# Linear attention and a two-layer MLP on one core: the hand-written order of chunks 0 to 2 is made anew

## The chip, the core and the metric

The kernel runs on one core of a Trainium2 chip. Its engines work side by side, each through its own instructions in order: TensorE (PE, matrix products into PSUM), VectorE (DVE), ScalarE (ACT), GpSimd (POOL, which also issues some of the DMAs) and SyncE (SP, which issues the other DMAs). An engine waits where its next instruction needs something that another engine or a transfer has not yet delivered. The metric is the device time of one execution in microseconds (us): 216.57 us is the median of three timed runs (216.57 to 217.8).

## The reference

Two stages, the second on the first's output (4 batches, 8 heads, 768 positions, head size 64; the MLP has 3072 tokens, 512 inputs and 2048 hidden columns):

```python
for b in range(nb):                       # blocks of 64 positions, one after the other
    intra = einsum('bhic,bhjc->bhij', qb, kb) * Dmask          # lam ** (i - j), 0 above the diagonal
    intra = einsum('bhij,bhjd->bhid', intra, vb)
    inter = einsum('bhid,bhde->bhie', qb * lam_pow, kv_state)
    out[:, :, sl] = intra + inter
    kv_state = lam_block * kv_state + einsum('bhsd,bhse->bhde', kb * rev_pow, vb)
h = x @ w_in                              # x: out, heads side by side, 3072 x 512
g = maximum(h, 0.0) + alpha * minimum(h, 0.0)
return g @ w_out                          # 3072 x 512
```

All inputs and the output are float32; the kernel multiplies in float16.

## The kernel before

**Chunks and units.** The work is cut into six chunks `c` of 512 tokens: 256 positions (two blocks of 128) of two batches `bi`. `pb = c // 2` is the place in the sequence; chunks 0 and 1 hold the first positions of all four batches. A chunk has four attention units (`units`, numbered 4c to 4c+3): batch 0 or 1 of the chunk, with the first or the second four heads. So units 4 to 7 are chunk 1: 4 and 5 of its first batch, 6 and 7 of its second.

**A unit's steps.** `load` (line 80) brings q, k or v of one batch of a chunk (0.5 MB, or half of it) from HBM, issued on SP. `cast` (line 261) makes float16 of it for one unit; a letter names the engine: A is ACT, V is DVE, G is POOL. `key_decayed` (line 274) multiplies k by its decay. `transposes` (line 291) brings q and k head size first: eight PE transposes and a copy from PSUM bank tk, or, with "D", one DMA transpose issued on SP. `transposed` (line 317) does q or k alone. `decayed` (line 335) multiplies the transposed q by its decay. `cluster(old, new)` (line 350) is PE's part: the inter and intra products of unit `old` and the scores and the state of unit `new`, then DVE's masked scores `sm`, the state update (R on ACT or DVE, RD on ACT for the first positions and on POOL later) and the copy of the output into `xT`. Either side may be absent.

**The MLP's steps.** `up(c, f)` (line 474) is four matmuls of 512 columns that make 128 of the 2048 hidden columns for a chunk, then ACT's `m` (line 487) and DVE's product `g` (line 503, at once, or later by `slope_product`). It needs all four units' `xT` and a quarter of w_in (`f // 4`). `down(c, t, part, 4)` (line 512) is four of the sixteen matmuls for 128 output tokens; `part` is the quarter of w_out that it reads. Behind the last part ACT copies the sum (line 531) and SP stores it, at once or by `store_held`.

**PSUM.** Banks by name: "h" (two), "op", "tk", and others for the clusters. A new user of a bank waits until the earlier one's readers are done.

**Weights.** `load_win(i)` (line 95) and `load_wout(i)` (line 101) bring a quarter of w_in or w_out, cast to float16 on the way, and are issued on POOL, where they stand in order with its casts and products. `gate` (line 109) is a tiny DMA on SP that reads one element of a weight quarter: SP waits in it until that quarter has landed, and so holds back the loads behind it:

```python
w = w_in_sb[0:1, 0, i * 512 : i * 512 + 1] if which == "in" else w_out_sb[0:1, 4 * i, 0:1]
nc.sync.dma_start(out=gates16[:, x : x + 1], in_=w)
```

**The order.** It is written out by hand, line by line, from line 595 on: the opening (chunk 0's attention, with `fill` matmuls of no use to the result that keep PE at work), then chunk 0's `up` and `down` with chunk 1's attention between, then chunk 1's `up` with chunk 2's attention. From line 817 a loop over chunks weaves the rest: `up` of chunk c and `down` of chunk c - 1 alternate, with the attention of chunk c + 1 spread among them.

```python
for c in range(2, NC):
    ...
    for f in range(NF):
        moe.append(lambda f=f: up(c, f))
        moe.append(lambda f=f: down(c - 1, f // 4, f % 4, 4))
    weave(att, moe)
```

The last chunk's `down` stands at the end (`down_last`).

Of the kernel before, what the change touches and what calls it, by code (L numbers as in the profile page):

```python
# [11 lines left out]
def kernel(  # L12
# [24 lines left out]
    B, H, S, D = q.shape  # L37
# [3 lines left out]
    NC = (S // W) * 2  # L41
# [88 lines left out]
    def fill(n, bank="h", zeros=None, w=CH):  # L130

        t = bank_of(bank, "unread")
        for i in range(n * CH // w):
            if w < CH:
                x = ident if zeros is None else zeros[:, 0:128]
                nc.tensor.matmul(t[:, ds(i * w % CH, w)], lhsT=x, rhs=x[:, 0:w], start=True, stop=True)
                continue
            if zeros is not None:
                nc.tensor.matmul(t, lhsT=zeros[:, 0:128], rhs=zeros, start=True, stop=True)
                continue  # L140
            nc.tensor.matmul(
                t.rearrange("p (a j) -> p a j", a=4),
                lhsT=ident,
                rhs=ident.unsqueeze(1).to_broadcast([128, 4, 128]),
                start=True,
                stop=True,
            )
# [322 lines left out]
    G = {}  # L470
# [3 lines left out]
    def up(c, f, bi=None, bank="h", later=False):  # L474
        h_ps = bank_of(bank, "h_ps")
        n = CH if bi is None else W
        for gi in range(NHP):
            x = XT[c][:, gi]
            nc.tensor.matmul(  # L479
                h_ps[:, 0:n] if bi is None else h_ps[:, 0:n].rearrange("p (e j) -> p e j", e=2),  # L480
                lhsT=w_in_sb[:, gi, ts(f, 128)],
                rhs=x.rearrange("p e b j -> p (e b j)") if bi is None else x[:, :, bi, :],
                start=(gi == 0),
                stop=(gi == NHP - 1),
            )
# [191 lines left out]
    up(0, 1, None, "op")  # L677
    up(0, 4, None, "tk", True)
    slope_product(0, 4, None)
    up(0, 3, None, "h", True)  # L680
    key_decayed(4, "G")
    slope_product(0, 3, None)
    cast(5, "k16", "G")
    up(0, 6, None, "h", True)
    up(0, 2, None, "op")
    up(0, 7, None, "tk")
    slope_product(0, 6, None)
    cast(4, "q16", "A")
    up(0, 5, None, "h")
    up(0, 8, None, "op")  # L690
    up(0, 11, None, "tk")
    up(0, 10, None, "h")
    load_wout(1)
    cast(4, "v16", "A")
    gate(3, "in")
    up(0, 14, None, "h")
    up(0, 15, None, "op")
    up(0, 13, None, "h")
    transposes(4, "V", False)
    decayed(4, "P")  # L700
    gate(1, "out")
    up(0, 9, None, "h")
    up(0, 12, None, "op")
# [6 lines left out]
    cast(6, "k16", "G")  # L710
    down(0, 2, 0, 4, "op")
    cast(6, "q16", "V")
    load_wout(2)
    transposes(6, "A", False)
    key_decayed(5, "G")
    down(0, 0, 1, 4, "h")
    load(2, 0, "k", None)
    cast(5, "v16", "V")
    key_decayed(6, "V")
    cast(7, "q16", "A")  # L720
    down(0, 2, 1, 4, "op")
    decayed(6, "G")
    load(2, 0, "q", None)
    cast(7, "k16", "V")
    load_wout(3)
    cluster(4, 5, "V", state_first=True)
    load(2, 1, "k", None)
    cast(8, "q16", "G")
    transposes(7, "A", False)
    decayed(5, "V")  # L730
    down(0, 3, 1, 4, "h")
    down(0, 3, 2, 4, "h")
    cast(9, "q16", "G")
    cast(6, "v16", "V")
    down(0, 2, 2, 4, "op")
    decayed(7, "V")
    cluster(5, 6, "A", state_first=True)
    key_decayed(8, "G")
    down(0, 1, 0, 4, "tk")
    down(0, 1, 1, 4, "tk")  # L740
    down(0, 1, 2, 4, "tk")
    key_decayed(7, "V")
    load(2, 0, "v", None)
    cast(8, "k16", "V")
    key_decayed(9, "V")
    transposes(8, "D", False)
    cast(9, "v16", "G")
    cast(7, "v16", "A")
    cluster(6, 7, "V", state_first=True)
    down(0, 0, 2, 4, "h")  # L750
    down(0, 0, 3, 4, "h")
    key_decayed(10, "V")
    cast(9, "k16", "G")
    load(2, 1, "q", None)
    down(0, 2, 3, 4, "op", True)
    cluster(7, None, "A")
    cast(8, "v16", "V")
    transposes(9, "D", False)
    cast(10, "k16", "G")
    down(0, 3, 3, 4, "h", True)  # L760
    up(1, 0, None, "h")
    query_decay(1, 0)
    store_held(0, 3)
    decayed(8, "G")
    up(1, 12, None, "op", True)
    slope_product(1, 12, None)
    up(1, 6, None, "h", True)
    slope_product(1, 6, None)
    load(2, 1, "v", None)
    cluster(None, 8)  # L770
    key_decayed(11, "G")
    query_decay(2, 0)
    decayed(9, "G")
    up(1, 1, None, "h", True)
    slope_product(1, 1, None)
    cast(11, "k16", "A")
    up(1, 7, None, "op", True)
    cast(10, "q16", "A")
    transposes(10, "D", False)
    slope_product(1, 7, None)  # L780
    cast(11, "q16", "A")
    down(0, 1, 3, 4, "tk")
    up(1, 13, None, "h", True)
    load(3, 0, "q", None)
    cluster(8, 9, "A")
    transposes(11, "D", False)
    slope_product(1, 13, None)
    load(3, 0, "k", None)
    decayed(10, "G")
    up(1, 2, None, "tk", True)  # L790
    slope_product(1, 2, None)
    up(1, 3, None, "op")
    store_held(0, 2)
    cast(10, "v16", "A")
    up(1, 15, None, "h", True)
    cluster(9, 10, "A")
    slope_product(1, 15, None)
    up(1, 10, None, "tk", True)
    load(3, 0, "v", None)
    cast(11, "v16", "A")  # L800
    load(3, 1, "k", None)
    slope_product(1, 10, None)
    up(1, 11, None, "h")
    up(1, 9, None, "op", True)
    decayed(11, "G")
    cluster(10, 11, "A")
    up(1, 5, None, "tk")
    up(1, 14, None, "h")
    slope_product(1, 9, None)
    up(1, 4, None, "h", True)  # L810
    slope_product(1, 4, None)
    cluster(11, None, "A")
    load(3, 1, "v", None)
    load(3, 1, "q", None)
    up(1, 8, None, "tk")
# [42 lines left out]
```

## Time and profile before

| What | Value |
|---|---|
| Timed runs, median | 216.57 us |
| The profiled execution | 215.89 us, span 214.1 us |
| Granted clock of TensorE | 0.999 |
| PE busy | 205.5 us, 96% of the span |
| DVE, ACT, POOL busy | 61%, 54%, 41% |
| HBM read and written | 27.27 MB, 6.29 MB |
| First `up` matmul | 20.20 us |
| Last of PE's matmuls starts | 210.6 us |

How to read it: times in the timeline count from the start of the span. A row gives start and length, the engine, the line of the kernel, the operation, what is written and read, and the number of instructions of the row; brackets give the idle time ahead of the first and what ended it. "q" behind an engine's name is its sequencer, which issues a DMA or waits. A DMA's landing is when its completion was seen, which is later than its last packet. Matmuls are pipelined, so the length of a row of them goes a little beyond the start of the next one; PE's pace is read from start to start (0.216 us for 512 columns). Queue q0 carries the loads that POOL issues (the weights), q1 those of SP. The shares of the DMA queues are of 16 DMA engines, and go over 100% where packets overlap.

### The profile page before, as it was taken

What the parts mean: (1) busy time and instruction counts of PE and PEld (TensorE: products, weight loads), DVE (VectorE), ACT (ScalarE), POOL (GpSimd) and SP (SyncE); (2) the same over time, 40 slices, a digit from 0 to 9 for tenths busy, and PEclk for the clock granted to TensorE, in tenths of its full rate; (3) what the DMA queues carried; (4) which work ended last, traced back from release to release, by engine and by line L of the source; (5) the groups of instructions that cost most, each with busy time, mean ns of one, the idle gap of its engine ahead of it and who ended that gap; (6) DMA issues with size and microseconds to landing.
All of it is one profiled execution on the core that took longest, in us unless ns stands there. A gap on an engine that the chain in (4) does not pass through costs nothing.

```text
span 214.1 us, 5232 instructions
## 1 busy us (share of the span) xinstructions
PE 205.5 (96%) x2093; PEld 107.5 (50%) x2093; DVE 129.6 (61%) x254; ACT 115.6 (54%) x218; POOL 87.7 (41%) x163
## 2 busy tenths in 40 slices
PE   7779997999999999999999999999999999999993
PEld 7455444555455444555554554554554444444453
DVE  7867689487799947676655655655546344444000
ACT  6978687245787654646554554644534543444121
POOL 8175056203775644976967357358301000000000
PEclk9999999999999999999999999999999999999999
DMA  5999999999999999699387786044011101110212
GB/s 148 298 277 194 226 299 218 183 263 261 218 207 296 316 221 259 166 239 230 77 210 183 198 222 173 0 101 98 5 49 49 39 13 51 49 49 3 98 49 98
DMA packets 62478, 33.90 MB, mean 158 GB/s; under 512 B 18150, under 2 KB 59510, under 8 KB 62454
## 3 DMA queue, kind: packets, MB, share of 16 engines
q1 hardware_dynamic: 58182, 29.37, 54.2%
q0 software_dynamic: 4224, 4.19, 12.0%
q8 instruction: 16, 0.26, 0.5%
q14 instruction: 8, 0.07, 0.1%
q10 hardware_dynamic: 48, 0.01, 0.0%
HBM read 27.27 MB, written 6.29 MB: 157 GB/s over the span
## 4 chain that ended last, share of the span: by engine, by line
PE 72%; DMA 20%; POOL 3%; SPq 2%; issue 1%; ACT 1%; ACTq 0%; POOLq 0%
PE h_ps L479 30%; PE o_ps L518 29%; DMA w_out_sb<-in_moe_w_out_dram 8%; PE o_ps L547 6%; DMA w_in_sb<-in_moe_w_in_dram 4%; DMA kraw<-in_k_dram 3%; DMA vraw<-in_v_dram 3%; PE s L384 2%; DMA qkT<-qk 2%; PE acc L396 2%; PE acc L367 2%; SPq L87 1%; POOL qk L252 1%; POOL qdT L340 1%; PE acc L411 1%
## 5 line engine op out<-in xcount | busy, mean ns | idle before, releaser
L503 DVE SCALAR_TENSOR_TENSOR g<-m,oma,h_ps 128x512 f16<-128x512 f32 (+1 forms) x97 | 70.6, 741 | 58.0 <-ACT m L487 57.1
L479 PE MATMUL h_ps<-xT,w_in_sb 128*128 128x512 f16 (+1 forms) x388 | 94.8, 377 | 0.0
L487 ACT ACTIVATE m<-h_ps 128x512 f32<-128x512 f32 (+1 forms) x97 | 57.3, 592 | 57.8 <-PE h_ps L479 55.1
L518 PE MATMUL o_ps<-w_out_sb,g 128*128 128x512 f16 x320 | 80.9, 379 | 1.2 <-DMA w_out_sb<-in_moe_w_out_dram 1.1
L479 PEld LDWEIGHTS <-w_in_sb 128*128 128x128 f16 x388 | 37.1, 98 | 43.0
L518 PEld LDWEIGHTS <-g 128*128 128x128 f16 x320 | 30.2, 98 | 36.2 <-issue 1.6
L422 DVE TENSOR_TENSOR sm<-s,dmask 128x512 f16<-128x512 f32 x48 | 30.8, 683 | 5.4 <-PE s L384 5.0
L461 POOL COPY RD<-R 64x128 f16<-64x128 f16 x64 | 18.5, 288 | 36.3 <-DVE R L447 33.8
L340 POOL TENSOR_TENSOR qdT<-qkT,qdecay 128x512 f16<-128x512 f16 (+1 forms) x20 | 21.2, 1062 | 12.4 <-ACT qkT L248 5.7
L531 ACT ACTIVATE o_sb<-o_ps 128x512 f32<-128x512 f32 (+2 forms) x26 | 14.7, 564 | 16.9 <-PE o_ps L547 10.9
L248 ACT ACTIVATE xT<-acc 128x512 f16<-128x512 f32 x22 | 13.1, 596 | 10.4 <-PE acc L411 7.2
L278 POOL TENSOR_TENSOR kdec<-kraw,kdecay 128x512 f16<-128x512 f32 x17 | 17.8, 1045 | 0.1
L252 POOL CAST qk<-kraw 128x512 f16<-128x512 f32 x20 | 12.1, 610 | 11.1 <-DMA kraw<-in_k_dram 10.3
L547 PE MATMUL o_ps<-w_out_sb,g 128*128 128x512 f16 (+2 forms) x96 | 14.1, 308 | 0.0
L447 DVE SCALAR_TENSOR_TENSOR R<-R,rdecay,acc 128x64 f16<-128x64 f16 x56 | 12.3, 273 | 0.0
L252 POOL CAST v<-vraw 128x512 f16<-128x512 f32 x14 | 8.8, 627 | 5.9 <-DMA vraw<-in_v_dram 5.9
L547 PEld LDWEIGHTS <-g 128*128 128x128 f16 x96 | 8.1, 98 | 6.1
L248 ACT ACTIVATE qk<-qraw 128x512 f16<-128x512 f32 x17 | 10.5, 623 | 0.3 <-DMA qraw<-in_q_dram 0.3
L384 PE MATMUL s<-qkT 64*64 64x128 f16 x384 | 10.0, 222 | 0.3 <-DMA qkT<-qk 0.3
L396 PE MATMUL acc<-sm,v 64*64 64x128 f16 x384 | 9.9, 217 | 0.0
L367 PEld LDWEIGHTS <-RD 128*128 128x128 f16 x80 | 6.3, 98 | 5.6 <-ACT RD L443 0.6
L367 PE MATMUL acc<-qdT,RD 128*128 128x128 f16 x80 | 8.4, 219 | 0.0
(68 smaller groups left out, 111.3 us busy)
## 6 DMA issues: line engine op xcount, KB each, us to landing
out_dram<-o_sb SPq DMA_DIRECT2D x23, 256.0 KB, 2.3
qraw<-in_q_dram SPq DMA_DIRECT2D x10, 512.0 KB, 7.1
kraw<-in_k_dram SPq DMA_DIRECT2D x10, 512.0 KB, 9.3
vraw<-in_v_dram SPq DMA_DIRECT2D x10, 512.0 KB, 8.1
w_in_sb<-in_moe_w_in_dram POOLq DMA_DIRECT2D x4, 512.0 KB, 8.2
w_out_sb<-in_moe_w_out_dram POOLq DMA_DIRECT2D x4, 512.0 KB, 7.8
kraw<-in_k_dram SPq DMA_DIRECT2D x4, 256.0 KB, 4.3
qraw<-in_q_dram SPq DMA_DIRECT2D x4, 256.0 KB, 5.5
```

Source lines behind the costliest of these rows:

```text
L248: nc.scalar.activation(out, in_, AF.Copy)
L252: nc.gpsimd.tensor_copy(out=out, in_=in_)
L278: engine(eng).tensor_tensor(out=kdec, in0=kr, in1=kdecay[:, ds(4 * hh, 4), :].rearrange("p h e -> p e h").unsqueeze(3).to_broadcast([128, ...
L340: engine(eng).tensor_tensor(out=qdT[:, :, :, p], in0=(t["qps"] if eng == "P" else t["qkT"][:, 0])[:, :, :, p], in1=qdecay[:, hh, :, :, p], ...
L367: nc.tensor.matmul(ot[a][:, hp, :].rearrange("p (e j) -> p e j", e=2), lhsT=RD[bb, ho][:, a, hp].rearrange("p h d -> p (h d)"), rhs=to["qd ...
L422: nc.vector.tensor_tensor(out=sm, in0=s[hl], in1=mask_of(hl, hh), op=ALU.mult)
L461: nc.gpsimd.tensor_copy(out=RD[b, hh][p, a, :, hl, :], in_=R[b, hh, 2 * pb + a][p])
L479: nc.tensor.matmul(h_ps[:, 0:n] if bi is None else h_ps[:, 0:n].rearrange("p (e j) -> p e j", e=2), lhsT=w_in_sb[:, gi, ts(f, 128)], rhs=x ...
L487: nc.scalar.activation(m[:, 0:n], h_ps[:, 0:n], AF.Relu, scale=-1.0)
L503: nc.vector.scalar_tensor_tensor(out=g, in0=mv, scalar=oma[:, f : f + 1], in1=hv, op0=ALU.mult, op1=ALU.add)
L518: nc.tensor.matmul(o_ps, lhsT=lhs(c, f, t), rhs=w_out_sb[:, f, :], start=(f == 0), stop=(f == NF - 1),)
L547: nc.tensor.matmul(o_ps[:, 0:n], lhsT=lhs(c, f, t), rhs=w_out_sb[:, f, ds(x, n)], start=(f == 0), stop=(f == NF - 1),)
```

## The change

Up to `cluster(3, None)`, the last of chunk 0's attention, one thing changes: four `fill` matmuls ahead of `cluster(0, 2)` write PSUM bank "tk" where they wrote "h". Behind it the written list is another one, and it goes on through chunk 2's `up`, so that the weaving loop starts at chunk 3. In it:

- chunk 0's first `up` is whole (it was done in two halves, by batch), and the sixteen come in another order;
- unit 4's q and k are transposed apart, its decayed q is made on POOL; many casts and products go to other engines or places;
- `load_wout(0)` stands behind two casts of q and a decayed q on POOL, and ahead of the key products; `load_wout(1)`, (2) and (3) stand in a row behind a cast of unit 7's k. They were spread among POOL's casts before;
- on SP, chunk 1's loads come all six ahead of the gate on w_out's second quarter (five before); chunk 2's loads stay behind it, in another order and with all but its last v ahead of the first DMA transpose;
- chunk 1's `down` parts of three of its four token blocks stand in a row behind its `up`, and chunk 2's `up` comes behind them, with chunk 3's attention and the start of chunk 4's in between. Loads of chunks 3 and 4 are placed to fit.

PE's instructions and the transfers are the same in kind and number but for the halves of the first `up`. The diff, cut (of the removed lines only those ahead of chunk 1's first cluster, and of the new ones all to the first cluster of chunk 2, then some):

```diff
     load_win(1)
-    fill(4, "h")
+    fill(4, "tk")
     cluster(0, 2, "A", own=True)
...
     cluster(3, None, "A")
-    up(0, 0, 0, "tk")
+    up(0, 3, None, "h")
+    up(0, 2, None, "op")
+    up(0, 0, None, "tk")
+    up(0, 1, None, "h")
+    up(0, 6, None, "h", True)
+    cast(4, "q16", "G")
+    transposed(4, 0, "A", "op")
+    decayed(4, "G")
     load(1, 0, "v", None)
-    cast(4, "k16", "G")
+    slope_product(0, 6, None)
+    cast(5, "q16", "G")
     load(1, 1, "k", None)
+    up(0, 7, None, "tk", True)
+    slope_product(0, 7, None)
+    up(0, 4, None, "h", True)
+    slope_product(0, 4, None)
     load_wout(0)
+    up(0, 11, None, "op")
+    key_decayed(4, "G")
+    up(0, 8, None, "tk")
+    key_decayed(5, "G")
+    up(0, 10, None, "h")
+    cast(4, "k16", "A")
+    up(0, 14, None, "h")
+    cast(4, "v16", "G")
     load(1, 1, "q", None)
-    up(0, 0, 1, "h", True)
-    slope_product(0, 0, 1)
...
-    load_wout(1)
-    cast(4, "v16", "A")
-    gate(3, "in")
...
-    gate(1, "out")
...
-    cluster(None, 4)
-    cast(5, "q16", "G")
-    transposes(5, "A", False)
-    down(0, 0, 0, 4, "h")
-    load(1, 1, "v", None)
...
+    cast(7, "k16", "G")
+    cast(5, "k16", "V")
+    up(0, 5, None, "op", True)
+    load_wout(1)
+    slope_product(0, 5, None)
+    load(1, 1, "v", None)
+    load_wout(2)
+    gate(1, "out")
+    transposed(4, 1, "A", "tk")
+    up(0, 13, None, "h")
+    up(0, 15, None, "h")
+    transposes(5, "A", False)
+    cluster(None, 4)
+    up(0, 9, None, "op", True)
+    slope_product(0, 9, None)
+    up(0, 12, None, "h", True)
+    cast(6, "k16", "A")
+    load_wout(3)
+    down(0, 0, 0, 4, "h")
+    cast(5, "v16", "G")
+    slope_product(0, 12, None)
+    gate(3, "in")
+    cluster(4, 5, "V", state_first=True)
+    cast(6, "q16", "G")
+    transposes(6, "A", False)
+    key_decayed(6, "G")
+    down(0, 2, 0, 4, "op")
+    load(2, 0, "k", None)
+    down(0, 3, 0, 4, "h")
+    cast(7, "q16", "G")
+    transposes(7, "V", False)
+    decayed(7, "V")
+    decayed(5, "V")
+    down(0, 2, 1, 4, "op")
+    cast(6, "v16", "V")
+    cast(8, "k16", "G")
+    key_decayed(7, "V")
+    down(0, 3, 1, 4, "h")
+    cluster(5, 6, "A", state_first=True)
+    decayed(6, "V")
+    cast(7, "v16", "A")
+    load(2, 1, "q", None)
+    cast(11, "q16", "G")
+    down(0, 1, 0, 4, "tk")
+    down(0, 2, 2, 4, "op")
+    down(0, 0, 1, 4, "h")
+    load(2, 0, "q", None)
+    cast(9, "k16", "G")
+    cast(8, "q16", "G")
+    cluster(6, 7, "A")
+    load(2, 1, "k", None)
+    key_decayed(10, "G")
+    down(0, 0, 2, 4, "h")
+    query_decay(2, 0)
+    down(0, 2, 3, 4, "op")
+    down(0, 1, 1, 4, "tk")
+    down(0, 1, 2, 4, "tk")
+    cluster(7, None, "A")
+    key_decayed(8, "V")
+    down(0, 1, 3, 4, "tk", True)
+    load(2, 0, "v", None)
+    cast(8, "v16", "G")
+    key_decayed(9, "G")
+    up(1, 6, None, "op")
+    transposes(8, "D", False)
+    load(3, 0, "k", None)
+    down(0, 0, 3, 4, "h", True)
+    down(0, 3, 2, 4, "h")
+    store_held(0, 0)
...
+    up(1, 5, None, "tk", True)
...
+    up(1, 7, None, "op", True)
...
+    up(1, 13, None, "h")
+    cast(10, "q16", "G")
+    down(0, 3, 3, 4, "h")
+    cluster(None, 8)
+    store_held(0, 1)
...
+    load(2, 1, "v", None)
+    cluster(8, 9, "A")
...
+    up(1, 9, None, "tk")
+    cast(10, "v16", "A")
...
+    cluster(9, 10, "V")
+    up(1, 14, None, "tk")
+    key_decayed(13, "V")
+    down(1, 2, 0, 4, "h")
...
+    down(1, 1, 3, 4, "op")
...
+    cluster(11, 12, "A")
+    down(1, 0, 3, 4, "h", True)
+    store_held(1, 0)
+    up(2, 7, None, "tk", True)
...
+    transposes(13, "D", False)
...
+    store_held(1, 3)
 
-    for c in range(2, NC):
+    for c in range(3, NC):
```

More of the change, by code (lines that the diff above doesn't have):

```diff
@@ L779 @@
+    up(1, 11, None, "h")
+    load(2, 1, "v", None)
+    cluster(8, 9, "A")
     transposes(10, "D", False)
[L780 to L783, printed above, removed]
-    load(3, 0, "q", None)
[L785 to L798, printed above, removed]
-    load(3, 0, "v", None)
-    cast(11, "v16", "A")
-    load(3, 1, "k", None)
[L802 to L811, printed above, removed]
@@ new lines @@
+    load(4, 0, "k", None)
+    down(1, 1, 0, 4, "op")
+    cast(12, "q16", "G")
+    cast(13, "k16", "A")
+    down(1, 1, 1, 4, "op")
+    key_decayed(11, "V")
+    cluster(10, 11, "V", state_first=True)
+    transposes(12, "D", False)
+    decayed(12, "V")
+    cast(15, "k16", "A")
+    cast(15, "q16", "G")
+    load(4, 1, "v", None)
+    load(3, 1, "v", None)
+    key_decayed(14, "G")
+    down(1, 1, 2, 4, "op")
+    down(1, 1, 3, 4, "op")
+    cast(14, "v16", "G")
+    cast(13, "v16", "V")
+    down(1, 2, 3, 4, "h", True)
@@ new lines @@
+    transposes(14, "D", False)
+    up(2, 2, None, "tk", True)
+    slope_product(2, 2, None)
+    cast(16, "k16", "A")
+    down(1, 3, 2, 4, "h")
+    up(2, 6, None, "h", True)
+    decayed(14, "G")
+    slope_product(2, 6, None)
+    cast(16, "q16", "G")
+    cast(17, "q16", "A")
+    down(1, 3, 3, 4, "h", True)
+    key_decayed(16, "G")
+    load(4, 0, "v", None)
+    cast(16, "v16", "A")
+    cluster(13, 14, "A")
+    cast(15, "v16", "G")
+    up(2, 1, None, "op", True)
+    up(2, 10, None, "h", True)
@@ new lines @@
+    slope_product(2, 1, None)
+    transposes(15, "D", False)
+    decayed(15, "G")
+    slope_product(2, 10, None)
+    store_held(1, 2)
+    load(4, 1, "k", None)
+    up(2, 11, None, "h")
+    cluster(14, 15, "A")
+    up(2, 4, None, "h")
+    cast(17, "k16", "A")
+    up(2, 8, None, "tk")
+    up(2, 9, None, "op")
+    transposes(16, "D", False)
+    decayed(16, "G")
+    up(2, 15, None, "h")
+    transposes(17, "D", False)
+    cluster(15, None, "A")
+    key_decayed(18, "G")
+    up(2, 5, None, "h")
@@ L818 @@
+    cluster(None, 16)
+    load(4, 1, "q", None)
+    cast(18, "k16", "A")
+    up(2, 14, None, "tk", True)
+    slope_product(2, 14, None)
+    cast(18, "v16", "G")
+    key_decayed(17, "G")
+    cast(17, "v16", "A")
+    cast(18, "q16", "G")
+    store_held(1, 3)
+    for c in range(3, NC):
         att = []
```

130 lines of the change are left out of this document (47 added, 83 removed).

## The prediction

> **What bounds it now.** I read the page's parts 1 and 2 first, then TensorE's (PE's) timeline, the list of waits, the chain that ended last, and the DMA queues in short windows.
>
> ```profile
> PE 205.5 (96%) x2093; PEld 107.5 (50%) x2093; DVE 129.6 (61%) x254; ACT 115.6 (54%) x218; POOL 87.7 (41%) x163
> ...
> PE   7779997999999999999999999999999999999993
> ...
> DMA  5999999999999999699387786044011101110212
> ```
>
> PE is full in nearly every slice, and DMA in the first 16 (5.35 us each). The granted clock was 0.999. So only PE's waits can be won, and they lie early:
>
> ```profile
> 12.43 1.02 PE L141 MATMUL unread<-ident 128*128 128x512 f16 x4 [0.99 <-ACT R L444]
> ...
> 20.20 12.36 PE L479 MATMUL h_ps<-xT,w_in_sb 128*128 128x256 f16 x60
> ...
> 37.00 2.75 PE L518 MATMUL o_ps<-w_out_sb,g 128*128 128x512 f16 x12 [1.12 <-DMA w_out_sb<-in_moe_w_out_dram]
> ...
> 50.11 3.00 PE L518 MATMUL o_ps<-w_out_sb,g 128*128 128x512 f16 x12
> ...
> 65.28 0.42 PE L384 MATMUL s<-qkT 64*64 64x128 f16 x16 [0.28 <-DMA qkT<-qk]
> ```
>
> Columns: start, length, what, and in brackets the idle time before it and what ended it. The fill at 12.43 idles 0.99 us for a PSUM bank. The sixty matmuls from 20.20 are chunk 0's `up` steps, back to back. At 37.00 PE waits 1.12 us for w_out's first quarter. At 50.11 twelve matmuls take 3.00 where twelve others (46.61) take 2.76: 0.24 us for w_out's last quarter. After 66 us nothing over 0.1 us follows. The chain tells why w_out was late:
>
> ```profile
> 22.17 6.85 DMA kraw<-in_k_dram
> 29.15 0.55 POOL qk L252
> 29.70 7.25 DMA w_out_sb<-in_moe_w_out_dram
> 37.00 2.75 PE o_ps L518 x12
> ```
>
> POOL, which issues w_out's loads in its own order, stood in a cast for chunk 1's first k until 29.15; its DMA then took 7.25 us to land.
>
> **PE's ledger.** An `up` or a quarter of a `down` (four matmuls) costs 0.864 us, eight transposes 0.46, a cluster of chunk 0 or 1 with both sides 0.90 (41.76 to 42.66), one without the old side 0.47, one without the new 0.55. The changed list reaches `down(0,2,1)`, the first use of w_out's second quarter, after 16 `up` (13.82), the transposes of units 4 to 7 (1.83), two clusters (1.37) and three `down` quarters (2.6): 19.6 us of PE work. The kernel before had done that same work at 41.39: the 40.03 of its timeline plus one cluster (0.90) and one transpose (0.46) that came a little later. Behind 41.39 it still waits 0.24, 0.28 and some 0.2 in small pieces: 0.7. So, if S is when the changed kernel starts `down(0,2,1)` and X are its waits behind that,
>
> change = S - 41.39 - 0.7 + X.
>
> **The fill bank.** `fill(4)` in bank tk needs not wait for ACT's R copy: tk's last copy ended at 10.4. Its 0.99 us goes, and what comes next does not take its place: unit 0's masked scores (DVE's sm) end at 12.24, its RD copies at 12.08, unit 2's v16 at 12.89, and its four matmuls need 0.87. Followed on through DVE's sm (1.29 per unit) and ACT's RD copies (0.55), `cluster(3)` ends about 19.1 instead of 20.20. Bounds: nothing (if POOL's casts, tied to loads landing at 12.96, hold the chain) to 1.2; I take 1.1.
>
> **First `up` whole.** The two half-wide steps of `up(0,0)` hid the copy of unit 3's xT (ACT, 0.60, at 20.30): PE lost 0.09. Now `up(0,3)` can do two of four matmuls (0.43) and waits until 0.75 behind the cluster: 0.3 lost. PE's own due time for `down(0,2,1)` is thus 19.1 + 0.3 + 19.6 = 39.0, and about 39.4 with small waits for banks (15's bank needs 14's product on DVE).
>
> **When w_out's second quarter lands.** This is the term that decides. POOL's order is now: `load_win(2)`, `load_win(3)`, cast of q 4 (landed 16.83), decayed 4, cast of q 5, `load_wout(0)`, two key products, cast of v 4, **cast of k 7, which waits for chunk 1's second k**, then `load_wout(1)`, (2), (3).
> - decayed 4 waits for ACT's copy of `transposed(4,0)`: five `up` behind 19.1 give 23.7, PE 0.2, ACT's m and copy 1.2, so 24.9; decayed 0.65 and cast 0.55: `load_wout(0)` is issued at 26.1, 3.6 earlier than now. It lands at 33.4 (with the 7.25 above) to 35.3 (with the 9.18 that the last quarter took beside other loads); PE wants it at 34.7. The 1.12 us goes, or up to 0.6 stays.
> - But now it moves while chunk 1's second k moves. That k landed at 32.62 with nothing beside it. How two queues share is shown here (queue 0 carries w_in and w_out, queue 1 all else; packets, MB, share):
>
> ```profile
> q0 software_dynamic: 401, 0.41, 80.2%
> q1 hardware_dynamic: 452, 0.23, 37.5%
> ```
>
> That is 46 to 49 us, w_out's last quarter against chunk 2's loads: queue 1 gets 0.08 MB per us, against 0.30 alone (27 to 31 us: 1.18 MB). The quarter's packets start 2.5 to 3.4 us after its issue, so at 28.6 to 29.5. k 7's 0.52 MB would be through at about 30.5 alone (w_in's last quarters, issued a us earlier, let queue 1 start some 0.5 earlier); by 29.5 to 30.4 it has 0.2 to 0.45 MB, and the rest crawls. It lands between 33.1 and 34.8; I take 34.0, the middle, since the two starts are equally near to rows.
> - cast 0.55, then w_out's second quarter: 34.55 + 7.25 = **41.8**. That is later than PE's 39.0 to 39.4, so S = 41.8, and the 1.1 us of the fill is spent waiting here. Waits on the way (w_out 0, v16 of unit 5, which stands behind the three issues on POOL at 0.76 each) are hidden in it.
>
> The Trainium skill, "DMA: Bandwidth & Descriptors", Anatomy of one DMA, gives 2.0 us plus bytes/436 GB/s for a load from this queue, an estimate of 4.4 us for a quarter's 1.05 MB read; by that the quarter would land at 39.0 and no wait would be left. The trace differs: its four w_out loads took 7.3 to 9.2.
>
> **SP's queue.** Chunk 1's last v is no longer behind the gate on w_out's second quarter, and every chunk 2 load is (the gate on w_in's last quarter moved behind it too; that quarter landed at 27.50 and holds nothing). The gate now opens at 41.8 (it was issued at 39.48 before). `cluster(None,8)` is due 17.0 us behind S (17 blocks of four, two clusters, one without a new side), and needs the DMA transpose of unit 8. Before, gate to landing took 16.9 (39.48 to 56.38) with five loads and one quarter of w_out; now there are five loads with two quarters still moving. If the cast of q 8 needs only its third load, it comes about 1.9 early; with a whole quarter's 2.5 added to 16.9 it comes 2.4 late. I take no wait, by the count of loads that it needs.
>
> **The rest, X.** Chunks 1 and 2 have the same instructions in a new order; chunk 1's `down` parts now stand in a row, without `up` beside them, which leaves DVE and ACT idle there and fuller before (16 products at 0.70 plus three clusters at 2.1 and two key products in 19 us, about full). ACT's cast of v 10 waits for a load that is behind two stores on SP, 0 to 0.8; unit 13's transpose behind two more stores, 0 to 0.6; DVE's lag against PSUM banks 0 to 0.3. X = 0.35, bounds 0 and 1.7. From chunk 3 on, nothing differs.
>
> **Sum.** 41.8 - 41.39 - 0.7 + 0.35 = +0.06 us. On the profiled execution's 215.89 (its span 214.1 and 1.8 around it) that is 215.95; the timed median, 216.57, stands 0.68 above that execution, so **216.6**. Its own range, with k 7 at 33.1 to 34.8 and X 0 to 1: -1.2 to +1.5, so 215.4 to 218.1.
>
> **Rivals.**
> 1. *The second quarter is in time* (0.22). If k 7 is not slowed (its packets ahead of w_out's, as at 32 to 33 us, where the hand-over cost it nothing), it lands at 32.0 and the quarter by 32.55 + 7.25 = 39.8; S is 39.4 to 39.8, X small, and the change -2.7 to -2.0: about 214.2. For it: the idle 0.99 and 1.12 are real, and PE has no other waits. Against: `load_wout(0)` is issued 3.6 us earlier, into queue 1's traffic. By the skill's figure above it would be this case.
> 2. *Chunk 2 starves, slower* (0.23). Queue 1 may get nothing at all beside two software loads. In 22 to 25 us
>
> ```profile
> q0 software_dynamic: 609, 0.61, 124.2%
> ```
>
> was all that moved, though SP had issued k and v from 22.17. With two quarters behind the gate, unit 8's transpose lands 2.4 late, and PE stands at `cluster(None,8)`. Price: +0.06 + 2.4 = +2.5, so 219.0; it decides once that landing is later than 17.0 behind the gate. The skill's same page, Queues, rings and completion order, has each DMA engine take turns between queues packet by packet: 46 to 49 us (401 against 452) agrees, 22 to 25 us does not. By the rule this rival would be out.
> 3. *The forecast* (0.55): w_out's second quarter sets S, and the wins are given back.
>
> Range: from rival 1's lower part, 213.9, to rival 2's 219.0; below it 0.06, above it 0.12. About 1% (2.2 us) is what a measurement tells from no change. Faster by over 1%, below 214.4: most of rival 1, 0.18. Slower, above 218.7: most of rival 2 and some of the forecast's upper end, 0.22. Within: 0.60.
>
> **What would show it.** Right: no idle before the fill near 11.4; first `up` at 19.1; `load_wout(0)` issued near 26; a PE wait on w_out_sb of 1 to 2.5 us near 40; no wait at 65. Wrong: a first `up` still at 20.2 (fill); no wait on w_out_sb (rival 1); a wait of PE on qkT or on v near 58 (rival 2); DVE or ACT holding PE between 55 and 72, which I cost at 0.3 and which has no row to bound it from above.

## The result and the profile after

The changed kernel takes **215.52 us** (median of 20 runs, 214.5 to 217.39) where the kernel before took 216.93 in the same measurement (20 runs, 215.95 to 218.86): a ratio of **0.9934, 95% interval 0.9913 to 0.9956**, 1.4 us less. The forecast was no change (216.6). The gain is within 1%, yet clear of its interval. Executions more than 1.5% above the fastest of their kernel are left out of the ratios below, and the single times of `wout0_late` and `before_no_d10`, profiled at granted clocks of 0.992 and 0.991, are not compared.

The page of the changed kernel: parts 1 and 2.

```profile
PE 206.4 (96%) x2089; PEld 107.3 (50%) x2089; DVE 131.6 (61%) x254; ACT 116.7 (54%) x220; POOL 86.8 (40%) x160
...
PE   7998997889999999999999999999999999999993
...
DMA  5999999999999999699549997043011011110212
```

PE's share is the same. Its second and third slice are fuller (9 and 9 for 7 and 7: the fill's wait is gone), and the dip after 32 us, one slice of 7 before, is now 7, 8, 8, so up to 48.5 us. What stands there is in PE's timeline of the changed kernel (columns: start, length, what, and in brackets the idle time before it and what ended it):

```profile
11.10 1.04 PE L141 MATMUL unread<-ident 128*128 128x512 f16 x4
...
19.68 4.49 PE L479 MATMUL h_ps<-xT,w_in_sb 128*128 128x512 f16 x20 [0.43 <-DMA w_in_sb<-in_moe_w_in_dram]
...
36.47 1.04 PE L518 MATMUL o_ps<-w_out_sb,g 128*128 128x512 f16 x4 [1.33 <-DMA w_out_sb<-in_moe_w_out_dram]
...
38.83 0.32 PE L411 MATMUL acc<-v,kdec 64*64 64x64 f16 x16 [0.64 <-POOL v L252]
...
42.28 1.89 PE L518 MATMUL o_ps<-w_out_sb,g 128*128 128x512 f16 x8 [0.33 <-DMA w_out_sb<-in_moe_w_out_dram]
...
46.59 1.89 PE L518 MATMUL o_ps<-w_out_sb,g 128*128 128x512 f16 x8 [0.65 <-DMA w_out_sb<-in_moe_w_out_dram]
```

The fill at 11.10 has no wait any more. A new one of 0.43 stands ahead of the first `up`: w_in's first quarter landed at 19.63. Then PE waits for w_out's first, second and third quarters and, between them, for unit 5's v. Unit 10's transpose landed at 70.28, and `cluster(9,10)` started at 71.95 without waiting for it. The start of `down(0,2,1)`, the prediction's S, is 42.28.

**This profile can't be set against that of before.** Its execution took 217.38 us, 1.9 above the changed kernel's median; the one of before took 215.89, 1.0 below its own. Their difference is +1.49, and that of the medians -1.41. A second profile of the changed kernel (`after_again` below; 215.79 us) shows in the same timeline:

```profile
20.04 4.49 PE L479 MATMUL h_ps<-xT,w_in_sb 128*128 128x512 f16 x20 [0.51 <-DMA w_in_sb<-in_moe_w_in_dram]
...
36.06 1.04 PE L518 MATMUL o_ps<-w_out_sb,g 128*128 128x512 f16 x4 [0.57 <-DMA w_out_sb<-in_moe_w_out_dram]
...
38.77 0.32 PE L411 MATMUL acc<-v,kdec 64*64 64x64 f16 x16 [0.99 <-POOL v L252]
...
41.73 1.89 PE L518 MATMUL o_ps<-w_out_sb,g 128*128 128x512 f16 x8
...
70.33 0.42 PE L384 MATMUL s<-qkT 64*64 64x128 f16 x16
```

The waits ahead of S come and go in size (0.57 or 1.33 for the first quarter), S is 0.55 earlier, no later quarter of w_out is waited for, and at 70.33 `cluster(9,10)` starts with unit 10's transpose in place (it landed at 68.27). In the kernel before that was the wait at 65.28.

**The prediction's ledger holds in every profile.** "Behind" is the sum of PE's waits after the start of `down(0,2,1)` (S), or in the old order after the point with the same work done (E), read from start to start of the matmuls:

| Execution | Order | Own time | E or S | Behind | Sum | Own time less sum |
|---|---|---|---|---|---|---|
| before | old | 215.89 | 41.39 | 0.77 | 42.16 | 173.73 |
| before_again | old | 217.82 | 42.12 | 1.94 | 44.06 | 173.76 |
| fill_only | old | 217.01 | 41.19 | 2.09 | 43.28 | 173.73 |
| after | new | 217.38 | 42.28 | 1.38 | 43.66 | 173.72 |
| after_again | new | 215.79 | 41.73 | 0.27 | 42.00 | 173.79 |
| list_only | new | 215.40 | 41.49 | 0.19 | 41.68 | 173.72 |

(`fill_only` and `list_only` are explained below: the old list with the new fill, and the new list with the old fill.) The last column is constant within 0.07 us, so these two terms are the whole difference, in one execution of an order against another of the same order too. E and S are at about the same place. What the new order has less of, in its two profiles near the median, is the waits behind them: 0.27 and 0.19, where the old order has 0.77 in its fastest profile and 1.94 and 2.09 in the others. The first profile of the changed kernel, 1.38, is the exception, and 0.8 of it is a wait for w_out's third quarter.

### The profile page after: what moved, and what is told of

Same layout as the page of the kernel before. It is cut to its first block, busy times and chain, and to the rows that moved or that the text cites. A ratio compares the mean times of both kernels' runs of the same rounds, so it can differ in the third digit from the quotient of the medians.

```text
span 215.6 us, 5212 instructions
## 1 busy us (share of the span) xinstructions
PE 206.4 (96%) x2089; PEld 107.3 (50%) x2089; DVE 131.6 (61%) x254; ACT 116.7 (54%) x220; POOL 86.8 (40%) x160
## 4 chain that ended last, share of the span: by engine, by line
PE 72%; DMA 20%; SPq 3%; POOL 2%; ACT 1%; issue 1%; DVE 0%; ACTq 0%
PE o_ps L518 30%; PE h_ps L479 29%; PE o_ps L547 6%; DMA vraw<-in_v_dram 5%; DMA kraw<-in_k_dram 5%; DMA w_in_sb<-in_moe_w_in_dram 5%; DMA w_out_sb<-in_moe_w_out_dram 5%; PE s L384 2%; PE acc L396 2%; SPq L87 2%; PE acc L367 2%; PE acc L411 1%; POOL qk L252 1%; ACT o_sb L531 0%; POOL w_in_sb L96 0%
## 5 line engine op out<-in xcount | busy, mean ns | idle before, releaser
L503 DVE SCALAR_TENSOR_TENSOR g<-m,oma,h_ps 128x512 f16<-128x512 f32 x96 | 70.5, 745 | 55.7 <-ACT m L487 54.2
L479 PE MATMUL h_ps<-xT,w_in_sb 128*128 128x512 f16 x384 | 93.4, 379 | 0.6 <-DMA w_in_sb<-in_moe_w_in_dram 0.4
L487 ACT ACTIVATE m<-h_ps 128x512 f32<-128x512 f32 x96 | 56.9, 597 | 50.6 <-PE h_ps L479 49.0
L518 PE MATMUL o_ps<-w_out_sb,g 128*128 128x512 f16 x320 | 79.5, 379 | 2.3 <-DMA w_out_sb<-in_moe_w_out_dram 2.3
L479 PEld LDWEIGHTS <-w_in_sb 128*128 128x128 f16 x384 | 36.5, 98 | 43.5 <-DMA w_in_sb<-in_moe_w_in_dram 0.6
L518 PEld LDWEIGHTS <-g 128*128 128x128 f16 x320 | 30.3, 98 | 38.1 <-DMA w_out_sb<-in_moe_w_out_dram 1.8
L461 POOL COPY RD<-R 64x128 f16<-64x128 f16 x64 | 19.6, 306 | 41.0 <-DVE R L447 39.3
L340 POOL TENSOR_TENSOR qdT<-qkT,qdecay 128x512 f16<-128x512 f16 (+1 forms) x19 | 20.1, 1059 | 11.8 <-ACT qkT L248 6.0
L278 POOL TENSOR_TENSOR kdec<-kraw,kdecay 128x512 f16<-128x512 f32 x16 | 17.2, 1075 | 3.0 <-DMA kraw<-in_k_dram 3.0
L252 POOL CAST qk<-kraw 128x512 f16<-128x512 f32 x12 | 7.4, 613 | 14.1 <-ACT RD L443 9.7
L252 POOL CAST qk<-qraw 128x512 f16<-128x512 f32 x13 | 8.0, 616 | 2.2 <-DMA qraw<-in_q_dram 2.0
```

The costliest lines, as they stand in the source:

```text
L252: nc.gpsimd.tensor_copy(out=out, in_=in_)
L278: engine(eng).tensor_tensor(out=kdec, in0=kr, in1=kdecay[:, ds(4 * hh, 4), :].rearrange("p h e -> p e h").unsqueeze(3).to_broadcast([128, ...
L340: engine(eng).tensor_tensor(out=qdT[:, :, :, p], in0=(t["qps"] if eng == "P" else t["qkT"][:, 0])[:, :, :, p], in1=qdecay[:, hh, :, :, p], ...
L461: nc.gpsimd.tensor_copy(out=RD[b, hh][p, a, :, hl, :], in_=R[b, hh, 2 * pb + a][p])
L479: nc.tensor.matmul(h_ps[:, 0:n] if bi is None else h_ps[:, 0:n].rearrange("p (e j) -> p e j", e=2), lhsT=w_in_sb[:, gi, ts(f, 128)], rhs=x ...
L503: nc.vector.scalar_tensor_tensor(out=g, in0=mv, scalar=oma[:, f : f + 1], in1=hv, op0=ALU.mult, op1=ALU.add)
```

## The experiments

The theories were: A, S is set by w_out's second quarter behind chunk 1's second k, as predicted; B, the gain is the fill's; C, the gain lies behind S, where the old order waits for more than its first profile showed.

### The same two kernels once more

No edit: another execution of each, the changed one with its times.

> The kernel before once more, for a second profile: the first one ran 215.89 us, 1.0 under its median of 216.93. Theory A: a run nearer the median has longer waits for w_out (1.12 at 37.0 and 0.24 at 50.8 in the first one), up by the 0.5 to 1.0 us that the run is longer. Theory B: the waits there are the same, and the time is lost elsewhere.

> The changed kernel once more, unchanged. Its first profile ran 217.38 us, 1.9 over its median of 215.52, and shows 4.7 us of PE waits behind the first up. If the run-to-run spread is in how late the weights land (theory A: the second quarter of w_out sets the start S of down(0,2,1)), a profile near the median shows the first up at 19.1 without a wait for w_in, S at 40.5 to 41.5 (42.28 in the first one), and PE waits of some 2.5 to 3.5 us in all. If the spread is elsewhere (theory B: in the clock, or behind 66 us), S stays near 42.2 and the time differs behind it. Time 0.991 to 0.996 of before.

The kernel before: 217.82 us. The changed one: 215.32 (12 runs), 0.992 of before (0.9883 to 0.9957). PE's timeline of the second profile of before:

```profile
22.95 10.53 PE L479 MATMUL h_ps<-xT,w_in_sb 128*128 128x512 f16 x48 [0.68 <-DMA w_in_sb<-in_moe_w_in_dram]
...
37.73 2.75 PE L518 MATMUL o_ps<-w_out_sb,g 128*128 128x512 f16 x12 [1.05 <-DMA w_out_sb<-in_moe_w_out_dram]
...
52.23 1.89 PE L518 MATMUL o_ps<-w_out_sb,g 128*128 128x512 f16 x8 [0.35 <-DMA w_out_sb<-in_moe_w_out_dram]
...
67.18 0.42 PE L384 MATMUL s<-qkT 64*64 64x128 f16 x16 [1.17 <-DMA qkT<-qk]
```

The list that the prediction took for granted is one draw. The wait for unit 10's transpose is 1.17 here and was 0.28 there: the transpose was issued 1.0 us later (61.87 for 60.86) and took 5.3 us to land for 4.4. The fourth quarter of w_out costs 0.5 from start to start for 0.24, and the wait for w_in's second quarter (landed 22.90, where it was 21.37) is not in the first profile at all.

### The fill alone, the list alone

`fill_only`, from the kernel before:

```diff
-    fill(4, "h")
+    fill(4, "tk")
```

`list_only` is the changed kernel with that line put back.

> The kernel before with the fill's bank alone changed (four fill matmuls write tk, not h). Theory A: first up at 19.1 instead of 20.2, but w_out's first quarter is issued behind a cast that waits for chunk 1's k (29.15) and lands near 37 as before, so PE's wait there grows from 1.1 to about 2.2 us: time within 0.3 us of before (ratio 0.9985 to 1.0015). Theory B: the fill is the whole gain, 1.1 to 1.4 us: ratio about 0.994.

> The changed kernel with the fill's bank put back to h. Theory A: PE starts the first up a us later, but meets the second quarter of w_out at the same S, so the time is that of the changed kernel within 0.3 us: ratio to before 0.992 to 0.996. Theory B (the fill is the whole gain): ratio 0.998 to 1.002.

The fill alone: 216.89, ratio 0.9971 (0.9924 to 1.0018). The list alone: 215.70, ratio 0.9935 (0.9894 to 0.9977). PE's timeline of the fill alone:

```profile
21.99 10.53 PE L479 MATMUL h_ps<-xT,w_in_sb 128*128 128x512 f16 x48 [0.65 <-DMA w_in_sb<-in_moe_w_in_dram]
...
36.79 2.75 PE L518 MATMUL o_ps<-w_out_sb,g 128*128 128x512 f16 x12 [0.93 <-DMA w_out_sb<-in_moe_w_out_dram]
...
66.40 0.42 PE L384 MATMUL s<-qkT 64*64 64x128 f16 x16 [1.04 <-DMA qkT<-qk]
```

The opening is 0.8 us shorter (first `up` at 19.43, just behind w_in's first quarter, which landed at 19.39), and PE then waits for w_in's second quarter (landed 21.95) and for w_out's first, which POOL issues at 29.70 as before. The first `down` starts at 36.79 for 37.00. The fill's gain is spent on waiting, as the prediction had it. Its ratio alone does not settle B, since the whole change's 0.9934 lies in its interval too. But the list alone gives what the whole change gives, and the 0.998 to 1.002 that B had for it lies just outside its interval: B falls.

### What sets S: w_out's first quarter later

```diff
-    load_wout(0)
     up(0, 11, None, "op")
...
     cast(4, "v16", "G")
+    load_wout(0)
```

> The changed kernel with the load of w_out's first quarter issued behind POOL's cast of unit 4's v (near 32 us) instead of near 26.7. Theory A (the quarter slows chunk 1's second k, since both move at once): that k lands at 31.8 to 32.8 instead of 33.2 to 35.3; the first quarter lands near 39 and PE waits some 4 us for it at the first down, so the time grows by 2.5 to 3.5 us. Rival E (the k is late for another reason): it still lands at 33.2 or later.

One execution, 219.62 us. POOL's and PE's timelines:

```profile
31.81 0.79 POOL L102 DMA_DIRECT2D w_out_sb<-in_moe_w_out_dram  x1
32.60 0.62 POOL L252 CAST qk<-kraw 128x512 f16<-128x512 f32 x1
33.15 2.25 POOL L102 DMA_DIRECT2D w_out_sb<-in_moe_w_out_dram  x3
```

```profile
39.68 1.42 PE L518 MATMUL o_ps<-w_out_sb,g 128*128 128x512 f16 x4 [4.65 <-DMA w_out_sb<-in_moe_w_out_dram]
```

Chunk 1's second k lands at 32.50, as in the kernel before (32.62), against 35.26 in the first profile of the changed one, whose POOL shows the stand in front of that cast:

```profile
26.55 0.79 POOL L102 DMA_DIRECT2D w_out_sb<-in_moe_w_out_dram  x1
...
35.31 0.62 POOL L252 CAST qk<-kraw 128x512 f16<-128x512 f32 x1 [3.34 <-DMA kraw<-in_k_dram]
35.87 2.29 POOL L102 DMA_DIRECT2D w_out_sb<-in_moe_w_out_dram  x3
```

The late quarter costs more than it could win: the first `down` waits 4.65 us for it. It does not show that the early quarter is what slows the k, for in another profile with the early quarter (`v5_early` below, whose edit stands behind that issue and that load) the k was not slowed:

```profile
26.91 0.79 POOL L102 DMA_DIRECT2D w_out_sb<-in_moe_w_out_dram  x1
...
32.50 0.61 POOL L252 CAST qk<-kraw 128x512 f16<-128x512 f32 x1
```

The k landed at 32.45 there, 32.41 in `packed` and 32.60 in `after_cl9early`, with the quarter issued at 26.9 to 27.2; and at 35.1 to 35.3 in four others (the two profiles of the changed kernel, `v11_gate0`, `no_wout`), with the quarter issued at 26.2 to 26.9. What goes with it is how much the k's queue had moved when the quarter's packets came: at 29 to 31 us SP's queue moved 857 packets and the weights' 69 in `v5_early`, 532 and 159 in the first profile of the changed kernel. So the quarter slows the k in some executions of this order and not in others; why is open.

### Unit 5's v earlier, the weights earlier, the last v held back

`v5_early`, from the changed kernel:

```diff
+    cast(5, "v16", "G")
     cast(7, "k16", "G")
...
     down(0, 0, 0, 4, "h")
-    cast(5, "v16", "G")
```

`packed` has that, and w_out's second quarter ahead of the k that holds POOL, with `down(0,2,1)` ahead of unit 7's transposes, and unit 6's transposes two `down` steps later:

```diff
     cast(5, "v16", "G")
+    load_wout(1)
     cast(7, "k16", "G")
...
-    load_wout(1)
...
-    transposes(6, "A", False)
-    key_decayed(6, "G")
     down(0, 2, 0, 4, "op")
     load(2, 0, "k", None)
     down(0, 3, 0, 4, "h")
+    transposes(6, "A", False)
+    key_decayed(6, "G")
+    down(0, 2, 1, 4, "op")
     cast(7, "q16", "G")
```

`v11_gate0` is `v5_early` with chunk 1's last v behind a gate on w_out's first quarter:

```diff
+    gate(0, "out")
     load(1, 1, "v", None)
```

> The changed kernel with the cast of unit 5's v on POOL ahead of the cast that waits for chunk 1's second k, so that the three issues of w_out no longer stand before it. Its PE wait (0.64 and 0.99 us in two profiles) goes. Theory A: PE only arrives earlier at down(0,2,1) and waits there for w_out's second quarter, which lands at 41.5 to 42.2 as before: S and the time stay within 0.3 us of the changed kernel (ratio to before 0.991 to 0.9945). Rival F (PE's own chain sets S): the time falls by 0.6 to 1.0 us more, ratio 0.987 to 0.990.

> A version meant to beat both: as the one with unit 5's cast ahead, and w_out's second quarter is also issued ahead of the cast that waits for chunk 1's second k (near 32.5 instead of 35), with down(0,2,1) one step earlier and the transposes of units 6 and 7 one step later on PE. Theory A: the second quarter lands at 39.5 to 40.5, S (at equal work) falls by 1 to 1.5 us, and the time is 0.4 to 0.7 percent under the changed kernel (ratio to before 0.985 to 0.989). Rival G: chunk 1's second k and q are slowed by as much, PE waits for unit 6's transposes instead, and the time is that of the changed kernel or above (0.992 or more).

> A version meant to beat the changed kernel: the one with unit 5's cast ahead, and chunk 1's last v held behind a gate on w_out's first quarter, so that w_out's second quarter has the DMA engines to itself sooner. If S is set by how much the DMA engines have to move by then (theory A; packets of 0.5 MB take 1.75 us), S falls by 0.8 to 1.7 us to near 40.2, the last v lands near 42 and is just in time for cluster(5,6): ratio to before 0.985 to 0.990. If the v is late instead, PE waits there as long as it won: 0.991 to 0.995.

`v5_early`: 215.13, ratio 0.9923 (0.9886 to 0.9961). `packed`: 216.42, ratio 0.998 (0.9952 to 1.0007). `v11_gate0`: 217.30, one execution. PE's timeline of the three, in that order:

```profile
41.21 1.89 PE L518 MATMUL o_ps<-w_out_sb,g 128*128 128x512 f16 x8 [0.70 <-DMA w_out_sb<-in_moe_w_out_dram]
```

```profile
40.89 1.02 PE L518 MATMUL o_ps<-w_out_sb,g 128*128 128x512 f16 x4 [1.19 <-DMA w_out_sb<-in_moe_w_out_dram]
...
44.00 0.27 PE L367 MATMUL acc<-qdT,RD 128*128 128x128 f16 x2 [0.78 <-DVE qdT L340]
```

```profile
43.11 1.89 PE L518 MATMUL o_ps<-w_out_sb,g 128*128 128x512 f16 x8 [1.78 <-DMA w_out_sb<-in_moe_w_out_dram]
```

Taking away the wait for unit 5's v (0.64 and 0.99 above) brings nothing that can be measured beyond the changed kernel (0.9923 and 0.992 of before): PE then waits for w_out's second quarter instead, 0.70. Its time of landing hardly follows its issue:

| Execution | Chunk 1's second k landed | Quarter issued | Quarter landed |
|---|---|---|---|
| packed | 32.41 | 32.14 | 40.84 |
| v5_early | 32.45 | 33.06 | 41.17 |
| list_only | 33.18 | 33.79 | 41.45 |
| after_again | 35.21 | 35.82 | 41.62 |
| after | 35.26 | 35.87 | 42.24 |

Issued 3.7 us earlier it lands 1.4 earlier, where the prediction added a fixed 7.25 to the issue. That it stands behind the bytes already on their way is a reading that fits these rows; no run tests it. Only in `packed` did the edit move the issue ahead of the k; the other issue times follow when the k landed. In `packed` PE waited 1.19 for the quarter and then 0.78 for DVE's decayed q, and at equal work (unit 7's transposes, 0.46, still to come) `down(0,2,1)` was at about 41.35: more was lost than won. `v11_gate0` was worse in its execution: the quarter was issued at 35.80 and landed at 43.07. The gate opened only at 35.5, so the v was issued at 36.13, just behind the quarter, and moved beside it: at 39 to 42 us 413 packets of SP's queue and 412 of the weights', where the first profile of the changed kernel has 4 and 477.

### What w_out's loads cost in all

`no_wout`: quarters 2 to 4 of w_out are not loaded, and every `down` reads the first.

```diff
-                rhs=w_out_sb[:, f, :],
+                rhs=w_out_sb[:, f % 4, :],
...
-    load_wout(1)
...
-    load_wout(2)
-    gate(1, "out")
+    gate(0, "out")
...
-    load_wout(3)
```

> The changed kernel without the loads of w_out's second to fourth quarter: every down reads the first quarter in their place (that part of the computation is left out), and SP's gate waits for the first quarter. Theory A (the landing of w_out's second quarter sets S): S falls from 41.5 to 42.3 to PE's own due time, 39.5 to 40.5, and the time by 1.3 to 2.5 us, to a ratio of 0.981 to 0.987. Rival F (PE's chain or unit 5's v sets S): S stays at 41 or later, ratio 0.989 or more.

214.44, ratio 0.9897 (0.984 to 0.9954): beside the changed kernel's 0.992 and 0.9934 that is 0.5 to 0.8 us less, within the intervals. PE's timeline there:

```profile
37.79 0.40 PE L306 MATMUL tp<-ident,qk 128*128 128x128 f16 x4 [0.73 <-POOL qk L252]
```

S is 40.20, in the 39.5 to 40.5 that theory A had for it, against 41.5 to 42.3 with the loads: so the weights do hold S in this list, by 1.3 to 2.1 us. The time fell by less than the 1.3 to 2.5 us of that theory, though its interval reaches them. PE now waits for unit 6's q: chunk 1's own loads are next. The edit also opens SP's gate earlier, so that chunk 2's loads start near 37 us, and the runs don't part the two.

### The wait for unit 10's transpose

`before_no_d10`: in the kernel before, unit 10 takes unit 9's transposed q and k, and its DMA transpose is left out.

```diff
     cast(10, "q16", "A")
-    transposes(10, "D", False)
+    T[10]["qkT"] = T[9]["qkT"]
```

`before_d10`: the cast and the transpose are issued earlier in the kernel before.

```diff
     slope_product(1, 6, None)
+    cast(10, "q16", "A")
+    transposes(10, "D", False)
     load(2, 1, "v", None)
...
-    cast(10, "q16", "A")
-    transposes(10, "D", False)
```

`after_cl9early`: the cluster that needs the transpose stands three `up` earlier in the changed kernel.

```diff
+    cluster(9, 10, "V")
     up(1, 3, None, "tk")
...
-    cluster(9, 10, "V")
     up(1, 14, None, "tk")
```

> The kernel before without the DMA transpose of unit 10: unit 10's scores and decayed q are made from unit 9's transposed q and k (that part of the computation is left out). This takes the wait at cluster(9,10) away without moving any other instruction. Theory C (most of the changed list's gain is this wait, 1.1 to 1.24 us in two profiles of this order, 0.3 in the first): ratio 0.9945 to 0.997, no PE wait between 57 and 80 us above 0.3 us. Rival D (another load of chunk 2 is late at once): PE waits 0.7 us or more for unit 10's v or for ACT behind it, and the ratio is 0.998 or more.

> The kernel before, with unit 10's cast of q and its DMA transpose ahead of the load of chunk 2's last v instead of behind two more up steps. Theory C: the changed list wins because the kernel before waits 1.1 to 1.2 us for this transpose at cluster(9,10) in most runs (only 0.3 in its first profile). Then that wait is gone or below 0.3 us, nothing takes its place, and the time falls by 0.5 to 1.2 us (ratio 0.9945 to 0.998). Rival D: the win comes from the start of w_out's use alone (S); then PE meets another late load behind it (the last v, 1 us later) and the ratio is 0.999 to 1.003.

> The changed kernel with cluster(9,10) three up steps (2.6 us) earlier, ahead of up(1,3). Unit 10's transpose lands at 67.9 to 70.3 in this order of loads, and the cluster would come due near 66.5. Theory C (what the new list wins is that the cluster comes due later): a PE wait of 1.3 to 3.0 us for the transpose comes back, and the time rises by 1.2 to 2.8 us, to a ratio of 0.998 to 1.005. Rival H (the transpose comes when its cast allows, and lands earlier too): no wait, ratio 0.991 to 0.994.

- `before_no_d10`: 216.31, **ratio 0.9952 (0.9919 to 0.9985)**: 1.0 us of the old order's time, over the timed runs, goes with this one transpose. The prediction's own reading, 0.28, is not in that interval (0.3 to 1.8 us), though close to its end. The edit also takes a transfer away, which may be a part of it.
- `before_d10`: 218.48, ratio 1.007 (1.0035 to 1.0104). PE's timeline:

```profile
63.58 2.75 PE L479 MATMUL h_ps<-xT,w_in_sb 128*128 128x512 f16 x12 [1.24 <-ACT o_sb L531]
...
68.59 0.32 PE L411 MATMUL acc<-v,kdec 64*64 64x64 f16 x16 [1.46 <-ACT v L248]
```

  The wait for the transpose is gone, and two larger ones on ACT have come: the cast that moved stands in ACT's order ahead of that copy and waited 2.03 us for its load, and the last v of chunk 2, which SP now issues later, landed only at 67.89. Issued at this place, the transpose only hands the wait on.
- `after_cl9early`: 216.90, ratio 1.0002 (0.9959 to 1.0045), where the changed kernel is at 0.9934: the gain is gone. But the transpose is the smaller part of it. It landed at 66.95 and cost 0.2 from start to start. The larger wait is on DVE:

```profile
71.47 1.02 PE L479 MATMUL h_ps<-xT,w_in_sb 128*128 128x512 f16 x4 [1.02 <-DVE g L503]
```

  A PSUM bank was not free, since DVE's products were late. DVE's timeline shows what held them up, the cluster's own work, without a gap:

```profile
68.11 1.28 DVE L422 TENSOR_TENSOR sm<-s,dmask 128x512 f16<-128x512 f32 x2
69.31 0.68 DVE L250 CAST xT<-acc 128x512 f16<-128x512 f32 x1
69.91 0.85 DVE L447 SCALAR_TENSOR_TENSOR R<-R,rdecay,acc 128x64 f16<-128x64 f16 x4
70.67 2.06 DVE L503 SCALAR_TENSOR_TENSOR g<-m,oma,h_ps 128x512 f16<-128x512 f32 x3
```

  The first product behind it is the one that PE waited for. So the place of that cluster matters for two reasons, and this run doesn't price the one asked about.

**What follows.** C is carried by three things: the sums in the table of profiles, the transpose taken out of the old order (0.5%), and PE's waits at `cluster(9,10)`. The three profiles of the old order with that transpose in its place wait there 0.28, 1.17 and 1.04 us; none of the eight of the new order with the cluster in its place does. The new list starts `cluster(9,10)` at 70.33 where the old one wanted it at 65.0, while its transpose lands at 68.27 for 65.24: 5.3 us later against 3.0, and the rest is its margin.

## Why the prediction was right or wrong

- **Fill bank** (right in its size, and in that it is spent): its 0.99 us of waiting is gone, and alone it gives 0.9971, with 1 in the interval. What the prediction left out is the wait that came next, w_in's first quarter (landed 19.63 and 19.99, for 18.78 in the first profile of before and 19.39 in its second): the first `up` ran on from 19.68 and 20.04, not from 19.1. It is hidden ahead of S.
- **`load_wout(0)`** (right in place, wrong in length): issued at 26.55 and 26.91 for the 26.1 forecast; it landed at 36.42 and 36.02, 9.9 and 9.1 us behind its issue, past the upper end of 35.3. The wait of 0.57 to 1.33 that stayed is above the 0 to 0.6 forecast, and hidden too.
- **Chunk 1's second k** (right in kind): slowed to 35.2 and 35.3 in the two profiles of the changed kernel, past the 34.8 of the bound, and to 33.2 in `list_only`; in three variants it was not slowed at all (32.4 to 32.6).
- **S = 41.8** (right in its number, in part by luck): 42.28, 41.73 and 41.49. Two errors met: the k came up to 1.3 later than the 34.0 taken, and the quarter behind it took 5.8 and 6.4 us, not 7.25. PE also did not stand there for 1 to 2.5 us, as the prediction's sign of being right had it, but for 0.33, 0 and 0.59: the rest was waited ahead of it, for w_in's first quarter, w_out's first and unit 5's v. Without the last of these waits (`v5_early`) the quarter sets S all the same, at 41.21.
- The price from the Trainium skill, "DMA: Bandwidth & Descriptors", Anatomy of one DMA, was an estimate of 4.4 us for a quarter. The changed order's rows are 5.8 to 11.3 (w_out's fourth quarter in the first profile: 37.40 to 48.74), all above it, and S did not come at the 39.0 to 39.4 that it would have allowed.
- **"Behind 41.39 it still waits 0.24, 0.28 and some 0.2 in small pieces: 0.7": this step failed.** These were the waits of one execution of 215.89 us, 1.0 below its kernel's median. Two other profiles of that order have 1.94 and 2.09, above all in the transpose of unit 10 (1.1 to 1.2), and the timed runs without it say 1.0. The mean of the two profiles of before, 216.86 us, is close to its median and has 1.36.
- **X = 0.35** (held by its bounds, 0 to 1.7): 0.27 and 0.19 in the two profiles near the median, 1.38 in the first, 0.8 of that for w_out's third quarter, which the prediction had not named. DVE between 55 and 72, costed at 0.3, showed 0.22 at 69.91 in the first profile and nothing in the second.
- **The sum again, with terms near the medians**: S + X is 41.84 (mean of 42.00 and 41.68), E + its waits is 43.11 (mean of 42.16 and 44.06): -1.3 us, where the medians moved -1.4. Of the 1.3 between this and the forecast's +0.06, the waits of the kernel before make 0.66 (1.36 for 0.7), E makes 0.36 (41.75 for 41.39), and S + X 0.31 (41.84 for 42.15). The structure held. The first two come from taking one quick execution for the kernel: the prediction added the 0.68 between that execution and its median to the changed kernel too, as if both orders had it, while in the profiles here it stands in waits that the new order has less of.
- **Rival 1**, the second quarter in time: out, though its condition, a k that is not slowed, came true in three variants (32.4 to 32.6 for its 32.0). The quarter then took 7.7 to 8.7 us, not 7.25, and landed at 40.8 to 41.2: with w_out loaded whole, `down(0,2,1)` never started ahead of 40.89, and not at 39.4 to 39.8. That the changed kernel is faster, as this rival had it, has another reason. **Rival 2**, chunk 2 starves: out. The gate opened at 41.6 to 42.3, and `cluster(None,8)` had its transpose (58.97 in the second profile, 17.2 behind S, with no idle time ahead of it). The stretch that it rested on, 22 to 25 us, was a short one: at 25 to 27 us SP's queue had 749 packets in the kernel before, for the weights' 188.

**Left open**: why one execution of the same program has its weights 0.8 to 1.5 us later than another, what decides whether chunk 1's second k is slowed, and how often the changed kernel waits for w_out's third quarter as in its first profile.

## What to carry to other kernels

Where a forecast comes down to a difference of waits of 0.2 to 1 us, ask first where the profiled execution stands against its kernel's median: one that is a microsecond faster has the short waits, and those that a reorder removes are priced too low by it. A wait for a transfer should be read as "due within a few tenths", and its worth taken from bounds on both sides, not as its length in one execution. And a wait removed ahead of a point that a transfer sets is spent on waiting for that transfer; the gain lies in what is given more room behind it.

## What the runs showed of the hardware that was not expected

**Landing doesn't follow issue.** From issue to landing, w_out's first quarter took 7.05 to 7.44 us in three profiles of the old order (issued at 29.7 to 30.3). In the new one, beside more of chunk 1's loads, it took 9.1 to 9.9 in three (issued at 26.6 to 26.9) and 8.4 to 8.6 in four variants (at 26.9 to 27.2), and 7.8 in `no_wout` (at 26.2). The changed kernel's second quarter, issued behind it at 35.8, took 5.8 and 6.4.

**How the two queues share differs from execution to execution.** The DMA queues (packets, MB, share) at 31 to 34 us, with w_out's first quarter late (`wout0_late`):

```profile
q1 hardware_dynamic: 1682, 0.85, 108.2%
...
q0 software_dynamic: 1, 0.00, 0.2%
```

Alone, SP's queue moves 0.85 MB in 3 us. At 31 to 33 us, beside w_out's first quarter, in the first profile of the changed kernel:

```profile
q0 software_dynamic: 277, 0.28, 82.8%
q1 hardware_dynamic: 282, 0.14, 35.1%
```

Both have as many packets. That equal turn is what the Trainium skill, "DMA: Bandwidth & Descriptors", Queues, rings and completion order, says of queues on an engine. In the same stretch of `v5_early` it is not so, though chunk 1's last q and v were on their way since 27.2 and 28.8:

```profile
q0 software_dynamic: 352, 0.36, 111.8%
q1 hardware_dynamic: 76, 0.04, 8.4%
```

SP's queue has a fifth of the weights' packets there. The runs don't show why.

**One program, two lists of waits.** Profiles of the same order were up to 1.9 us (0.9%) apart at granted clocks of 0.997 to 1.000, and most of it was in the waits for transfers.
